# Wide moving operands on four column groups, paired key turns and a new reduction in a decode attention kernel

## The chip, the cores and the metric

The kernel runs on one core of a Trainium2 chip, in one launch. The metric is device time in microseconds; five runs of the kernel before have a median of 196.19 us.

## The reference

One token goes through two branches. Branch A is attention of 32 heads of 128 over the last 4096 positions of a key and a value cache; branch B is a small gated MLP. Both start from the layernorm of x, and every tensor is bf16.

```python
x = A_x                                   # (1, 1, 512)
xn = _layernorm(x)
q = xn @ wq                               # 32 heads x 128
scores = q . k[:, last 4096] * 128**-0.5  # k, v: (32, 32768, 128), the last 4096 rows of each
o = softmax(scores) . v[:, last 4096]
s = o @ wo                                # (4096, 512)
h = gelu(_layernorm(xn) @ w1)
hs = (quarters of h shifted along the sequence, which has length 1, so zeros) @ w2
x1 = xn + hs
h2 = gelu(_layernorm(x1) @ w3) @ w4       # w3 (512, 1376), w4 (1376, 512)
out = x + s * silu(x1 + h2)
```

The keys and values that are needed make 64 MiB of the 78.84 MB that the kernel reads.

## The kernel before

**Groups and rows.** The 32 heads are worked in eight groups g of G = 4 heads. A key or value tile of a group is 128 partitions by CP = 128 rows of 128 values, 4 MB: partition p holds 128 consecutive positions of one of the four heads, and which head it is goes by p modulo 4. A score is thus the product of a row c of partition p with the query of that partition's head.

**Two ways to a score.** VectorE takes the first nd(g) of the 128 rows of a group: it multiplies them with the query, spread over all partitions as q_bc, and sums (k_vector, L329 and L331, in four quarters of nd/4 rows). TensorE takes the rest in batches of up to eight: it transposes each row (k_turn, L345), ScalarE copies the batch out of PSUM (L347), and a matmul of the transposed keys with four queries gives four columns per row (k_scores, L353), of which ScalarE and VectorE pick the one of the partition's own head (sm_own, L362, and sm_max, L367). nd is 64 for groups 0, 1 and 7, 68 for group 3, and 80 for the others.

**Softmax.** The maximum of each partition (L369) is turned into a row (sm_turn, mt_ps, L375), reduced per head (mx, L377), negated into md (L379) and spread back (mb_ps, L384); ScalarE then makes the exponentials pT (L391) and their sums. A matmul with ones adds the sums over partitions (den_ps, L397) and VectorE takes the reciprocal rden (L402).

**Values.** For groups 0 to 6 (MOVED) the values are the moving operand: a matmul takes four rows of pT as 16 stationary columns and four rows of v as 512 moving columns (v_part, L431), at four row offsets of one PSUM tile ov, which a matmul with zeros opens (L427). ScalarE copies ov to SBUF (L435). Of each 16 by 512 block only the parts where the row of pT meets the same row of v count; v_add picks and adds them with eight matmul instructions against the 0/1 matrix fold (L447), and v_out multiplies with rden: on ScalarE (L461) for groups 0 to 4, on VectorE (L457) for the last three. For group 7 v is the stationary operand, one row at a time (L440), in parts as its four loads (cuts 0, 64, 96, 112, 128) arrive.

**Output rows.** The 32 head outputs go through wo in blocks of 16, 8, 4 and 4 heads. ox_spread and ox_pick (L468 to L482) regroup a block so that the rows of wo can lie 4 or more to a partition; y_wide (L495) multiplies the first block in one PSUM row, y_block and y_head (L156) the others into y_ps.

**The front.** The layernorm sums, the MLP (a_ps L236, a_bf, hr_ps L250 and L255) and the queries (qT_ps L271) come first, with the weights as stationary operand for a_ps and qT_ps. w4 is loaded as eight rows to a partition, 32 further rows, and two tiles of 160 rows each (w4_few) on 20 partitions.

**Order.** All loads go down SP's queue in program order: w2, w3, w4, wq, keys 0 to 2, values 0, keys 3, values 1, and so on. Three buffers hold keys (the first 24 rows of wo take one for a time), two hold values, so SP waits for the last reader of a buffer before it issues the next load. Step s of the main loop works the keys of group s, the softmax of group s - 1 and the values of group s - 2 (LAG); v_add of group s - 3 stands in it too. TensorE, VectorE and ScalarE are in a region in which they take their work strictly in the order of the program. In a step, VectorE's order is: quarter 0 of the keys, rden of group s - 2, quarter 1, mx and md of group s - 1, quarters 2 and 3, then the sum and maximum of L367 and L369. All small PSUM tiles of a step (den_ps, mt_ps, mb_ps, oT, ox_ps) share one buffer of ps_misc, so each waits until the one before has been read.

Of the kernel before, what the change touches and what calls it, by code (L numbers as in the profile page):

```python
# [8 lines left out]
P = 128  # L9
BF16 = mybir.dt.bfloat16  # L10
# [11 lines left out]
NE = 5  # L22
# [3 lines left out]
MOVED = (0, 1, 2, 3, 4, 5, 6)  # L26
# [3 lines left out]
def kernel(  # L30
# [28 lines left out]
    assert F == 8 * P + 64 * NE + 32  # L59
# [30 lines left out]
    w4_sb = wts.tile([P, 9, D], BF16, name="w4_sb")  # L90
    load(w4_sb[:, 0:8, :], B_w4[0:8 * P, :].rearrange("(p c) n -> p c n", p=P))
    load(w4_sb[0:32, 8, :], B_w4[F - 32:F, :])
    w4_few = wts.tile([64, 8, D], BF16, name="w4_few")
    nc.gpsimd.memset(w4_few[:], 0.0)
    for c in range(2):
        f0 = 8 * P + 32 * NE * c
        load(w4_few[32 * c:32 * c + 4 * NE],
             B_w4[f0:f0 + 32 * NE, :].rearrange("(b a t) n -> a b (t n)", b=4, a=NE))
# [4 lines left out]
    def load_kv(pool, cache, g, cuts=(0, CP)):  # L103
# [3 lines left out]
        for c0, c1 in zip(cuts, cuts[1:]):  # L107
# [11 lines left out]
    one_f = ones_f[0:1, 0:1]  # L119
    ones_bf = const.tile([P, P], BF16, name="ones_bf")  # L120
    nc.vector.memset(ones_bf[:], 1.0)

    sel = wts.tile([H, H // G, PB, G], BF16, name="sel")
    nc.vector.tensor_copy(out=sel[:], in_=ident_bf[0:H, 0:H].rearrange("k (i a) -> k i a", a=G).unsqueeze(2)
                          .to_broadcast([H, H // G, PB, G]))
# [21 lines left out]


# [33 lines left out]

    few = const.tile([P, 2, 32], BF16, name="few")
    nc.vector.memset(few[:], 0.0)
    for c in range(2):
        nc.vector.tensor_copy(
            out=few[:, c, 0:4 * NE].rearrange("p (a b) -> p a b", b=4),
            in_=ident_bf[:, 4 * NE * c:4 * NE * (c + 1)].rearrange("p (b a) -> p a b", b=4))

# [35 lines left out]
    def w3_cols(c, j):  # L225
        if j < 8:
            return w3_sb[:, c, j:8 * P:8]
        if j == 8:
            return w3_sb[:, c, F - 32:F]
        return w3_sb[:, c, 8 * P + j - 9:8 * P + 64 * NE:8]  # L230

    chunks = [P] * 8 + [32] + [8 * NE] * 8
    a_ps = ps_misc.tile([P, 17], FP32, tag="misc", name="a_ps")
    for j, m in enumerate(chunks):
        for c in range(KC):
            nc.tensor.matmul(a_ps[0:m, j:j + 1], lhsT=w3_cols(c, j), rhs=z3_bf[:, c:c + 1],  # L236
                             start=(c == 0), stop=(c == KC - 1))
    a_bf = small.tile([P, 17], BF16, name="a_bf")
    nc.scalar.activation(out=a_bf[:, 0:8], in_=a_ps[:, 0:8], func=ACT.Gelu_apprx_tanh)  # L239
    nc.scalar.activation(out=a_bf[0:32, 8:9], in_=a_ps[0:32, 8:9], func=ACT.Gelu_apprx_tanh)  # L240
    nc.scalar.activation(out=a_bf[0:8 * NE, 9:17], in_=a_ps[0:8 * NE, 9:17], func=ACT.Gelu_apprx_tanh)
    af_ps = ps_misc.tile([64, 8], FP32, tag="misc", name="af_ps")
    nc.tensor.matmul(af_ps[:], lhsT=few[0:8 * NE].rearrange("p a b -> p (a b)"), rhs=a_bf[0:8 * NE, 9:17],
                     start=True, stop=True)
    af_bf = small.tile([64, 8], BF16, name="af_bf")
    nc.vector.tensor_copy(out=af_bf[:], in_=af_ps[:])

    hr_ps = ps_misc.tile([1, D], FP32, tag="misc", name="hr_ps")
    for c in range(KC):
        nc.tensor.matmul(hr_ps[:], lhsT=shifted_bf[:, c:c + 1], rhs=w2_sb[:, c, :], start=(c == 0),  # L250
                         stop=False)
    for i, m in enumerate(chunks):
        act = a_bf[0:m, i:i + 1] if i < 9 else af_bf[:, i - 9:i - 8]
        w = w4_sb[0:m, i, :] if i < 9 else w4_few[:, i - 9, :]
        nc.tensor.matmul(hr_ps[:], lhsT=act, rhs=w, start=False,  # L255
                         stop=(i == len(chunks) - 1))
    hr = wts.tile([1, D], FP32, name="hr")
    nc.vector.tensor_copy(out=hr[:], in_=hr_ps[:])  # L258
    h2_ps = ps_misc.tile([P, P], FP32, tag="misc", name="h2_ps")
    rows_open(h2_ps)  # L260
    rows_add(h2_ps, one_f, hr, True)
# [6 lines left out]
    qT_ps = ps_misc.tile([P, H], FP32, tag="misc", name="qT_ps")  # L268
    for h in range(H):
        for c in range(KC):  # L270
            nc.tensor.matmul(qT_ps[:, h:h + 1], lhsT=wq_sb[:, c, h * Dh:(h + 1) * Dh],  # L271
                             rhs=xq_bf[:, c:c + 1], start=(c == 0), stop=(c == KC - 1))
    qT_bf = small.tile([P, H], BF16, name="qT_bf")
    nc.vector.tensor_copy(out=qT_bf[:], in_=qT_ps[:])
    qr_ps = ps_misc.tile([H, Dh], BF16, tag="misc", name="qr_ps")
    nc.tensor.transpose(qr_ps[:], qT_bf[:], ident_bf[:])
    q_rows = wts.tile([H, Dh], BF16, name="q_rows")
    nc.vector.tensor_copy(out=q_rows[:], in_=qr_ps[:])
    q_bc = small.tile([P, H // G, Dh], BF16, name="q_bc")
    for i in range(0, H // G, 4):  # L280
        qb_ps = ps_tr.tile([P, 4, Dh], FP32, tag="pt", name="qb_ps")
        for k in range(4):
            nc.tensor.matmul(qb_ps[:, k, :], lhsT=sel[:, i + k, :, :].rearrange("k b a -> k (b a)"),
                             rhs=q_rows[:], start=True, stop=True)
        nc.scalar.copy(out=q_bc[:, i:i + 4, :], in_=qb_ps[:])  # L285
# [29 lines left out]
    def nd(g):  # L315

        return 64 if g < EARLY or g >= LATE else 68 if g == 3 else 80
# [17 lines left out]
    def batches(g):  # L335
        n, m = nd(g), CP - nd(g)
        k = -(-m // 8)
        edges = [n + m * i // k for i in range(k + 1)]
        return list(zip(edges, edges[1:]))

    def k_turn(g, kn, b):
        c0, c1 = batches(g)[b]
        pt = ps_tr.tile([P, 8, P], BF16, tag="pt", name="pt")
        for c in range(c0, c1):
            nc.tensor.transpose(pt[:, c - c0, :], kn[:, c, :], ident_bf[:])  # L345
        kts[b] = kt_pool.tile([P, 8, P], BF16, tag="kt", name="kt")
        nc.scalar.copy(out=kts[b][:, 0:c1 - c0, :], in_=pt[:, 0:c1 - c0, :])  # L347

    def k_scores(g, b):
        kt = kts.pop(b)  # L350
        c0, c1 = batches(g)[b]
        for c in range(c0, c1):
            nc.tensor.matmul(st[g]["sT"][:, c - nd(g), :], lhsT=kt[:, c - c0, :],  # L353
                             rhs=qT_bf[:, G * g:G * g + G], start=True, stop=True)
# [68 lines left out]
    def v_part(g, v, c0=0, c1=CP):  # L423
        s = st[g]
        if g in MOVED:
            s["ov"] = ps_o.tile([P, 4, Dh], FP32, tag="oT", name="ov")
            nc.tensor.matmul(s["ov"][:], lhsT=zero_bf[:], rhs=zero_bf[:].unsqueeze(1).to_broadcast([P, 4, Dh]),  # L427
                             start=True, stop=False, skip_group_check=True)
            for i in range(CP // 4):
# [7 lines left out]
        if c0 == 0:  # L437
            s["oT"] = ps_o.tile([P, G], FP32, tag="oT", name="oT")
# [51 lines left out]
    def y_wide(i, t0, t1):  # L490
        n = blocks[i][1]
        if t0 == 0:
            yr[i] = ps_tr.tile([1, D], FP32, tag="pt", name="yr_ps")
# [146 lines left out]
```

## Time and profile before

| quantity | value |
|---|---|
| median of 5 runs (lowest, highest) | 196.19 us (195.1, 196.34) |
| profiled execution: its own time, its span | 196.3 us, 194.5 us |
| TensorE matmul, weight load, VectorE, ScalarE busy | 136.2, 96.7, 145.4, 90.2 us |
| mean granted clock of TensorE | 0.683 |
| read from memory | 78.84 MB |

Busy time is a sum over the whole span; which engine holds the end is read from the slices (the span in 40 parts of 4.9 us, a digit for the busy tenths), from the chain of work that ended last, and from the timeline of a stretch. In a group's row the columns are the line, engine, operation and tiles, the count, then busy time and mean duration, then idle time ahead of it with what ended it.

### The profile page before, as it was taken

The page shows a single profiled execution, that of the slowest core. Times are in us where ns is not written, and L with a number is a line of the kernel's source. Part 1 is how long each engine was busy: PE and PEld are TensorE (multiplying, and loading weights), DVE is VectorE, ACT ScalarE, POOL GpSimd, SP SyncE. Part 2 cuts the span into 40 slices and gives each one's busy share as a digit, 9 for nine tenths or more (in the row PEclk, how much of TensorE's full clock was granted, in tenths as well). Part 3 has the DMA queues.
Part 4 walks back from the last instruction along what each step waited for, and adds up shares of the span by engine and source line. Part 5 has one row for each costly group of instructions (what it writes and reads, how often), then busy time and mean ns, then how long its engine had stood idle before and what let it go on. Part 6 is the DMA issues. An engine that isn't in the chain of part 4 may idle for free.

```text
span 194.5 us, 3919 instructions
## 1 busy us (share of the span) xinstructions
PE 136.2 (70%) x1696; PEld 96.7 (50%) x1696; DVE 145.4 (75%) x168; ACT 90.2 (46%) x197; POOL 5.9 (3%) x12
## 2 busy tenths in 40 slices
PE   0548978876965169249767891974497989787892
PEld 0447248755855053248437451932493358536281
DVE  0580012999999999998999999999999997942011
ACT  2003002888678265308865850681378157843100
POOL 8210000000000000000000000000000000000000
PEclk9999975695555555855788567578555795855575
DMA  6999999999999999999999999999999999999950
GB/s 205 429 431 425 425 435 435 426 428 425 431 428 433 431 435 431 431 438 431 428 431 431 428 431 408 451 431 431 428 438 433 421 426 391 453 428 406 394 221 0
DMA packets 4722, 79.08 MB, mean 407 GB/s; under 512 B 666, under 2 KB 1210, under 8 KB 1722
## 3 DMA queue, kind: packets, MB, share of 16 engines
q1 hardware_dynamic: 4554, 78.84, 95.3%
q8 instruction: 13, 0.21, 0.4%
q10 hardware_dynamic: 152, 0.00, 0.0%
q14 instruction: 3, 0.02, 0.0%
HBM read 78.84 MB, written 0.00 MB: 405 GB/s over the span
## 4 chain that ended last, share of the span: by engine, by line
DVE 44%; PE 32%; DMA 13%; ACT 5%; issue 4%; POOL 0%; POOLq 0%; ACTq 0%; SPq 0%
DVE S L331 25%; DVE prod L329 14%; DMA kv<-in_A_k_cache_dram 11%; PE ov L431 5%; PE pt L345 4%; PE oT L447 4%; ACT kt L347 3%; PE hr_ps L255 3%; PE a_ps L236 2%; DMA x_bf<-in_A_x_dram 2%; PE yr_ps L495 2%; PE qT_ps L271 2%; PE oT L440 2%; PE sT L353 2%; PE y_ps L156 1%
## 5 line engine op out<-in xcount | busy, mean ns | idle before, releaser
L331 DVE TENSOR_REDUCE S<-prod 128x20 f32<-128x2560 bf16 (+2 forms) x32 | 82.2, 2570 | 1.1
L347 ACT COPY kt<-pt 128x1024 bf16<-128x1024 bf16 (+1 forms) x56 | 54.8, 1008 | 17.4 <-PE pt L345 16.7
L345 PE MATMUL pt<-ident_bf,kv 128*128 128x128 bf16 x444 | 47.7, 279 | 2.9 <-DMA kv<-in_A_k_cache_dram 2.8
L329 DVE TENSOR_TENSOR prod<-kv,q_bc 128x2560 bf16<-128x2560 bf16 (+2 forms) x32 | 43.5, 1360 | 1.8 <-ACT q_bc L285 1.3
L345 PEld LDWEIGHTS <-kv 128*128 128x128 bf16 x444 | 38.7, 128 | 7.5 <-DMA kv<-in_A_k_cache_dram 3.9
L353 PE MATMUL sT<-qT_bf,kt 128*128 128x4 bf16 x444 | 20.8, 169 | 15.0 <-ACT kt L347 14.1
L353 PEld LDWEIGHTS <-kt 128*128 128x128 bf16 x444 | 17.3, 104 | 22.7 <-ACT kt L347 22.4
L431 PE MATMUL ov<-kv,pT 128*16 128x512 bf16 x224 | 24.1, 608 | 0.0
L447 PE MATMUL oT<-fold,ov_sb 128*128 128x4 f32 x56 | 10.7, 315 | 14.5 <-DVE rden L402 13.6
L447 PEld LDWEIGHTS oT<-fold,ov_sb 128*128 128x128 f32 x56 | 10.1, 270 | 15.9 <-DVE rden L402 14.0
L391 ACT ACTIVATE pT<-S,mb 128x128 bf16<-128x128 f32 x32 | 14.0, 579 | 0.3
L431 PEld LDWEIGHTS <-pT 128*16 128x16 bf16 x224 | 6.8, 123 | 14.1 <-issue 13.8
L461 ACT ACTIVATE o<-oT,rden 128x1 bf16<-128x1 f32 x20 | 3.6, 264 | 20.3 <-PE oT L447 20.3
L435 ACT COPY ov_sb<-ov 128x512 f32<-128x512 f32 x7 | 4.1, 585 | 17.0 <-PE ov L431 17.0
L457 DVE TENSOR_TENSOR o<-oT,rden 128x4 bf16<-128x4 f32 x3 | 0.5, 161 | 11.9 <-PE oT L447 9.4
L362 ACT ACTIVATE own<-sT,par 128x48 f32<-128x48 f32 (+2 forms) x32 | 7.6, 360 | 3.6 <-PE sT L353 3.6
L391 ACT ACTIVATION_READ_ACCUMULATOR pT<-S,mb 128x1 f32 x32 | 8.4, 263 | 0.0
L239 ACT ACTIVATE a_bf<-a_ps 128x8 bf16<-128x8 f32 x1 | 0.2, 177 | 14.4 <-PE a_ps L236 14.4
L375 PE MATMUL mt_ps<-ident_f,m 128*1 128x128 f32 x8 | 3.0, 373 | 5.3 <-DVE rden L402 4.4
L258 DVE COPY hr<-hr_ps 1x512 f32<-1x512 f32 x1 | 0.7, 679 | 7.3 <-PE hr_ps L255 7.3
L384 PE MATMUL mb_ps<-md,par_t 5*128 5x4 f32 x16 | 4.1, 325 | 2.7 <-DVE md L379 2.7
L236 PE MATMUL a_ps<-z_bf,w_sb 128*128 128x1 bf16 (+2 forms) x68 | 4.8, 205 | 1.5 <-DVE z_bf L219 1.5
(119 smaller groups left out, 102.8 us busy)
## 6 DMA issues: line engine op xcount, KB each, us to landing
kv<-in_A_k_cache_dram SPq DMA_DIRECT2D x7, 4096.0 KB, 30.9
kv<-in_A_v_cache_dram SPq DMA_DIRECT2D x7, 4096.0 KB, 29.1
wq_sb<-in_A_wq_dram SPq DMA_DIRECT2D x1, 4096.0 KB, 16.3
kv<-in_A_k_cache_dram SPq DMA_DIRECT2D x2, 2048.0 KB, 20.5
wo<-in_A_wo_dram SPq DMA_DIRECT2D x1, 2048.0 KB, 25.8
kv<-in_A_v_cache_dram SPq DMA_DIRECT2D x1, 2048.0 KB, 10.2
w_sb<-in_B_w_dram SPq DMA_DIRECT2D x1, 1376.0 KB
w_sb<-in_B_w_dram SPq DMA_DIRECT2D x1, 1024.0 KB, 9.0
```

Of the source, the lines that this page charges most:

```text
L236: nc.tensor.matmul(a_ps[0:m, j:j + 1], lhsT=w3_cols(c, j), rhs=z3_bf[:, c:c + 1], start=(c == 0), stop=(c == KC - 1))
L255: nc.tensor.matmul(hr_ps[:], lhsT=act, rhs=w, start=False, stop=(i == len(chunks) - 1))
L329: nc.vector.tensor_tensor(out=prod[:, 0:m, :], in0=kn[:, rows, :], in1=q_bc[:, g:g + 1, :].to_broadcast([P, m, Dh]), op=ALU.mult)
L331: nc.vector.tensor_reduce(out=st[g]["S"][:, rows], in_=prod[:, 0:m, :], axis=AX.X, op=ALU.add)
L345: nc.tensor.transpose(pt[:, c - c0, :], kn[:, c, :], ident_bf[:])
L347: nc.scalar.copy(out=kts[b][:, 0:c1 - c0, :], in_=pt[:, 0:c1 - c0, :])
L353: nc.tensor.matmul(st[g]["sT"][:, c - nd(g), :], lhsT=kt[:, c - c0, :], rhs=qT_bf[:, G * g:G * g + G], start=True, stop=True)
L362: nc.scalar.mul(s["own"][:, 0:m, a], s["sT"][:, 0:m, a], par[:, a:a + 1])
L384: nc.tensor.matmul(mb_ps[:], lhsT=par_t[:].rearrange("k b a -> k (b a)"), rhs=md[:], start=True, stop=True)
L391: nc.scalar.activation(out=s["pT"][:, :, a], in_=s["S"][:], func=ACT.Exp, scale=scale, bias=mb[:, a:a + 1], accum_out=s["sum"][:, a:a + 1])
L431: nc.tensor.matmul(s["ov"][r:r + 4 * G], lhsT=s["pT"][:, c:c + 4, :].rearrange("p i a -> p (i a)"), rhs=v[:, c:c + 4, :], start=False, sto ...
L447: nc.tensor.matmul(s["oT"][:], lhsT=s["ov_sb"][:, j, :], rhs=fold[:, G * j:G * j + G], start=(j == 0), stop=(j == 3))
```

## The change

- w4 is loaded as ten rows to a partition and 96 further rows of one; w4_few and its picking matrix go.
- The MLP's products have the activations as the one stationary column and the weights as moving operand of up to 512 columns, at four row offsets (32 apart) of a PSUM tile that a matmul with zeros opens; the gelu is then taken of a row, and the row is turned into columns by three transposes. hr comes in four partial rows, which ind adds.
- Queries likewise: 32 matmuls of 512 columns, copied to q_row; q_bc comes from it by one matmul per four groups. For the keys in pairs, q_row is written twice beside itself, turned as fp32, and stored as q_pair, with zeros in the other key's four columns.
- k_turn reads two neighbouring key rows (2 x 128 bf16) as 128 fp32 values and turns them in one transpose against ident_f. k_scores multiplies the even and the odd halves with q_pair, two matmuls of eight columns for each pair, which add up.
- nd becomes 80 for group 3 and 72 for group 7.
- All groups use the wide form of values. v_add is four fp32 transposes into one ps_misc tile, 124 columns apart, and a reduction on VectorE. Of the last group, the first 64 rows go wide and are folded by v_fold, the rest follow one row at a time.
- Output blocks 0, 1 and 2 go wide at four row offsets; y_four and y_sum hold their partial rows, added through ind at the end.

The diff, cut to its core:

```diff
-    w4_sb = wts.tile([P, 9, D], BF16, name="w4_sb")
-    load(w4_sb[:, 0:8, :], B_w4[0:8 * P, :].rearrange("(p c) n -> p c n", p=P))
-    load(w4_sb[0:32, 8, :], B_w4[F - 32:F, :])
...
-    for c in range(2):
-        f0 = 8 * P + 32 * NE * c
-        load(w4_few[32 * c:32 * c + 4 * NE],
-             B_w4[f0:f0 + 32 * NE, :].rearrange("(b a t) n -> a b (t n)", b=4, a=NE))
+    w4_sb = wts.tile([P, 11, D], BF16, name="w4_sb")
+    load(w4_sb[:, 0:10, :], B_w4[0:10 * P, :].rearrange("(p c) n -> p c n", p=P))
+    load(w4_sb[0:96, 10, :], B_w4[10 * P:F, :])
...
+    def zeros(ps):
+        nc.tensor.matmul(ps, lhsT=zero_bf[:], rhs=zero_bf[:].unsqueeze(1).to_broadcast([P, ps.shape[1], P]),
+                         start=True, stop=False, skip_group_check=True)
...
+    a_ps = ps_misc.tile([P, 3, P], FP32, tag="misc", name="a_ps")
+    zeros(a_ps[:])
     for c in range(KC):
...
+        for j, dst, w in parts:
+            nc.tensor.matmul(dst, lhsT=z3_bf[:, c:c + 1], rhs=w, start=False, stop=(c == KC - 1),
+                             skip_group_check=True)
...
+    for i, (col, w) in enumerate(terms):
+        r = 32 * (i % 4)
+        nc.tensor.matmul(hr_ps[r:r + 1].rearrange("r j n -> r (j n)"), lhsT=col, rhs=w, start=False,
+                         stop=(i >= len(terms) - 4), skip_group_check=True)
...
+    for b in range(2):
+        zeros(qr[b][:])
         for c in range(KC):
...
+            for a in range(G):
+                nc.tensor.matmul(qr[b][32 * a:32 * a + 1], lhsT=xq_bf[:, c:c + 1], rhs=wc[:, 4 * b:4 * b + 4, a, :],
+                                 start=False, stop=(c == KC - 1), skip_group_check=True)
+    nc.scalar.copy(out=q_row[:, 0:4, 0, :], in_=qr[0][:])
+    nc.vector.tensor_copy(out=q_row[:, 4:8, 0, :], in_=qr[1][:])
...
-        return 64 if g < EARLY or g >= LATE else 68 if g == 3 else 80
+        return 64 if g < EARLY else 72 if g >= LATE else 80
...
-        pt = ps_tr.tile([P, 8, P], BF16, tag="pt", name="pt")
-        for c in range(c0, c1):
-            nc.tensor.transpose(pt[:, c - c0, :], kn[:, c, :], ident_bf[:])
-        kts[b] = kt_pool.tile([P, 8, P], BF16, tag="kt", name="kt")
-        nc.scalar.copy(out=kts[b][:, 0:c1 - c0, :], in_=pt[:, 0:c1 - c0, :])
+        n = (c1 - c0) // 2
+        pt = ps_tr.tile([P, 4, P], FP32, tag="pt", name="pt")
+        for i in range(n):
+            c = c0 + 2 * i
+            nc.tensor.transpose(pt[:, i, :], kn[:, c:c + 2, :].rearrange("p c d -> p (c d)").bitcast(FP32),
+                                ident_f[:])
+        kts[b] = kt_pool.tile([P, 4, 2 * P], BF16, tag="kt", name="kt")
+        nc.scalar.copy(out=kts[b][:, 0:n, :], in_=pt[:, 0:n, :].bitcast(BF16))
...
-        for c in range(c0, c1):
-            nc.tensor.matmul(st[g]["sT"][:, c - nd(g), :], lhsT=kt[:, c - c0, :],
-                             rhs=qT_bf[:, G * g:G * g + G], start=True, stop=True)
+        for i in range((c1 - c0) // 2):
+            c = c0 + 2 * i - nd(g)
+            for l in range(2):
+                nc.tensor.matmul(st[g]["sT"][:, c:c + 2, :].rearrange("p c a -> p (c a)"),
+                                 lhsT=kt[:, i, l::2], rhs=q_pair[:, g, l, :], start=(l == 0), stop=(l == 1))
...
+    def v_wide(g, v, c1=CP):
+        s = st[g]
+        for i in range(c1 // 4):
+            c, r = 4 * i, 32 * (i % 4)
+            nc.tensor.matmul(ov[r:r + 4 * G], lhsT=s["pT"][:, c:c + 4, :].rearrange("p i a -> p (i a)"),
+                             rhs=v[:, c:c + 4, :], start=(i < 4), stop=(i >= c1 // 4 - 4),
+                             skip_group_check=True)
+        s["ov_sb"] = sm_pool.tile([P, 4, Dh], FP32, tag="ov_sb", bufs=1, name="ov_sb")
+        nc.scalar.copy(out=s["ov_sb"][:], in_=ov[:])
 
     def v_add(g):
+        s = st[g]
+        ot_ps = ps_misc.tile([P, 4 * P], FP32, tag="misc", name="ot_ps")
+        step = P - 4
+        for j in range(4):
+            nc.tensor.transpose(ot_ps[:, step * j:step * j + P], s["ov_sb"][:, j, :], ident_f[:])
+        s["oT"] = sm_pool.tile([P, G], FP32, tag="oT", name="oT")
+        nc.vector.tensor_reduce(out=s["oT"][:], in_=ot_ps[:].rearrange("p (x m) -> p m x", m=32)[:, 0:G, :],
+                                axis=AX.X, op=ALU.add)
+
+    def v_fold(g):
         s = st[g]
         s["oT"] = ps_misc.tile([P, G], FP32, tag="misc", name="oT")
         for j in range(4):
             nc.tensor.matmul(s["oT"][:], lhsT=s["ov_sb"][:, j, :], rhs=fold[:, G * j:G * j + G],
-                             start=(j == 0), stop=(j == 3))
+                             start=(j == 0), stop=False)
...
+    def y_wide(i, last):
         n = blocks[i][1]
...
+        for t in range(n):
+            r = 32 * (t % 4)
+            nc.tensor.matmul(yr[0][r:r + 1].rearrange("r j n -> r (j n)"), lhsT=ox_blk[i][:, t:t + 1],
+                             rhs=wo_blk[i][:, t, :], start=False, stop=(last and t >= n - 4),
+                             skip_group_check=True)
...
             if s > 1:
                 sm_den(s - 2)
                 sm_rden(s - 2)
-            if h - 1 in MOVED:
+            if h > 0:
                 v_add(h - 1)
                 v_out(h - 1)
-            if s == 7:
-                rows_add(y_ps, one_f, y_row, False)
...
-            y_block(1)
-            v_part(h, v)
+            y_open()
+            y_wide(1, False)
+            v_wide(h, v)
             v_add(h)
             v_out(h)
             ox_spread(2)
         else:
-            v_part(h, v, 0, cuts[1])
+            v_wide(h, v, cuts[1])
             ox_pick(2)
-            y_block(2)
-            for c0, c1 in zip(cuts[1:], cuts[2:]):
+            y_wide(2, True)
+            nc.vector.tensor_tensor(out=y_sum[:], in0=y_four[:], in1=yr[0][:].rearrange("p j n -> p (j n)"),
+                                    op=ALU.add)
+            v_fold(h)
+            v_part(h, v, cuts[1], cuts[2])
+            rows_add(y_ps, ind, y_sum, False)
+            for c0, c1 in zip(cuts[2:], cuts[3:]):
                 v_part(h, v, c0, c1)
             v_out(h)
```

## The prediction, made before the result was known

> **What bounds the kernel now.** I read the slices of the page first, then the chain, then the timeline of VectorE and TensorE from the landing of the seventh key tile on. From the page:
>
> ```profile
> DVE  0580012999999999998999999999999997942011
> DMA  6999999999999999999999999999999999999950
> DVE S L331 25%; DVE prod L329 14%; DMA kv<-in_A_k_cache_dram 11%; PE ov L431 5%; PE pt L345 4%; PE oT L447 4%; ACT kt L347 3%; PE hr_ps L255 3%; PE a_ps L236 2%; DMA x_bf<-in_A_x_dram 2%; PE yr_ps L495 2%; PE qT_ps L271 2%; PE oT L440 2%; PE sT L353 2%; PE y_ps L156 1%
> L345 PE MATMUL pt<-ident_bf,kv 128*128 128x128 bf16 x444 | 47.7, 279 | 2.9 <-DMA kv<-in_A_k_cache_dram 2.8
> L447 PE MATMUL oT<-fold,ov_sb 128*128 128x4 f32 x56 | 10.7, 315 | 14.5 <-DVE rden L402 13.6
> ```
>
> Two things are full at once. The DMA engines are busy from 3 to 187 us, so bytes alone (78.84 MB at about 430 GB/s) hold the end near 188. VectorE is full from 33 to 171. The chain crosses from one to the other at the seventh key tile (group 6), which VectorE reaches just as it lands. The timeline of VectorE from there:
>
> ```profile
> 135.25 1.49 DVE L329 TENSOR_TENSOR prod<-kv,q_bc 128x2560 bf16<-128x2560 bf16 x1 [0.21 <-DMA kv<-in_A_k_cache_dram]
> 139.51 0.17 DVE L402 RECIPROCAL rden<-den_ps 128x4 f32<-128x4 f32 x1
> 139.63 1.49 DVE L329 TENSOR_TENSOR prod<-kv,q_bc 128x2560 bf16<-128x2560 bf16 x1
> 144.23 0.28 DVE L377 TENSOR_REDUCE mx<-mt_ps 1x4 f32<-1x128 f32 x1 [0.26 <-PE mt_ps L375]
> ...
> 158.84 0.18 DVE L402 RECIPROCAL rden<-den_ps 128x4 f32<-128x4 f32 x1 [0.30 <-PE den_ps L397]
> 163.44 0.28 DVE L377 TENSOR_REDUCE mx<-mt_ps 1x4 f32<-1x128 f32 x1 [0.99 <-PE mt_ps L375]
> 171.30 0.28 DVE L369 TENSOR_REDUCE m<-S 128x1 f32<-128x128 f32 x1
> ```
>
> VectorE goes from the reciprocal (L402) straight into its next quarter of keys: nothing stands between them. From group 6's keys to the last row maximum it needs 171.58 - 135.25 = 36.33 us, 1.55 of them idle (0.26 + 0.30 + 0.99). After that the timeline of TensorE shows a tail in which little overlaps:
>
> ```profile
> 139.74 1.87 PE L447 MATMUL oT<-fold,ov_sb 128*128 128x4 f32 x8 [1.94 <-DVE rden L402]
> 173.58 0.37 PE L375 MATMUL mt_ps<-ident_f,m 128*1 128x128 f32 x1 [0.27 <-DVE rden L402]
> 180.39 3.58 PE L431 MATMUL ov<-kv,pT 128*16 128x512 bf16 x32
> 184.66 1.06 PE L447 MATMUL oT<-fold,ov_sb 128*128 128x4 f32 x8 [0.69 <-ACT ov_sb L435]
> 188.37 1.87 PE L440 MATMUL oT<-pT,kv 128*128 128x4 bf16 x64
> ```
>
> **What the Trainium skill says.** *TensorEngine Tiling (Array Packing)*, Key Properties: tiles of the array run in parallel. The trace agrees: the 32 products of L431, each 512 columns wide and 634 ns long when slow, start 0.107 us apart in four row offsets. *DMA: Bandwidth & Descriptors*, "Why a DMA increments its semaphore by 16": a transfer uses the largest number of engines up to 16 that divides its slowest dimension on both sides, the lowest-numbered ones. The two w4_few loads (source dimension 5, 20 partitions) show five semaphore packets each in the DMA records, the other loads 16; after them wq finishes on most engines at 19.3 to 20.0 us and on five at 21.9 to 22.0. *TensorE: Matmul & The Clock Gate*, queue depth: VectorE takes its queue strictly in order; the trace has no VectorE instruction out of program order. The same page, Terms, calls the transpose mode four times faster for fp32. The trace has one fp32 transpose, mt_ps with a single stationary column; the next matmul starts 0.16 us behind it, so at least that form isn't slow.
>
> **The change, part by part.**
>
> *w4 evenly.* The two loads put 2 x 32 KB on five engines; spread out, it is 20 KB on each of 16. Those five lose 44 KB, at 26.9 GB/s (32 KB in 1.22 us) 1.6 us; the others gain 20 KB, 0.75 us. Since the rings never run empty, the skew lives to the end. For group 6's keys the semaphores come at 131.3 to 134.75; the five latest move to about 132 to 133.1, the latest of the others from 133.2 to 133.9. So tiles land some 0.8 us earlier (134.4 for 135.2 as VectorE sees it), and so does the last byte, 188.9 to 188.1.
>
> *Queries and MLP.* MLP products now take 13.1 to 25.9 us (68 of L236 in 4.8, 21 of L250 and L255 in 7.2). On four groups: 20 products of at most 384 columns, about 1.3 us, and 15 of 512, 15 x 0.107 = 1.6, with zeroing 0.4 each and a turn of the row about 1; done by 20. That is hidden by the wq load (about 21 once even). Queries: 32 products x 0.107 = 3.4 slow, half of it at full clock, I take 2.6; two zeroings 0.6, a copy 0.6, a broadcast 0.4, a copy 0.55 (q_bc takes 0.53 now): 26 at the earliest. The first half of group 0's keys lands at 26.9 less 0.8, seen 0.5 later. VectorE's first keys start near 27 instead of 33.45.
>
> *Rows of VectorE.* A quarter of 16 rows takes 3.58 us, 17 rows 3.66, 20 rows 4.3. Group 3 gains 12 rows: step 3 goes from 16.57 us (0.6 idle) to 18.14, as step 4 has it. Group 7 gains 8: 4 x (3.95 - 3.58) = 1.5 us.
>
> *The sum over the parts of a value row, v_add.* Eight L447 matmuls, 1.87 us at slow clock and 1.06 to 1.12 at full, read by ScalarE, become four fp32 transposes of 128 x 128 and a reduction **on VectorE**, placed right behind the reciprocal. The transposes need the one ps_misc buffer, which the denominator holds until that reciprocal has read it. So VectorE stands there with its next quarter of keys queued behind the reduction, waiting for TensorE, in steps 3 to 7. Price: L447's fp32 weight loads stand 0.213 us apart at slow clock. If the 0.16 of a fp32 moving operand hides beside the next load, four cost 3 x 0.213 + 0.37 = 1.0 us; if not, 3 x 0.373 + 0.37 = 1.5; at full clock about 0.65. I take 1.25, between the slow ones. With a reduction of 0.24 (ln_tot 0.16, mx 0.28) and two handovers of 0.06 (rden end to L447) the stop is d = 1.6 us, with bounds 1.0 and 1.85. Four times slower fp32 would make it 2.3 (four operands at 0.43 each); no row excludes that for 128 columns.
>
> *Keys in pairs.* Eight bf16 transposes and eight score matmuls make 1.25 us a batch at slow clock (step 7). Four fp32 ones at 0.213 to 0.373 are 0.85 to 1.5 instead of 0.86, scores and ScalarE's copy (1.0) unchanged. I take nothing for it: in steps 2 to 6 TensorE idles waiting for keys or the reciprocal, and in step 7 it has one batch less. If that cover is gone, 5 batches after the reciprocal cost 3 us.
>
> *VectorE's sum.* Start 27; step 0 to 41.9; step 1 waits for its tile (last semaphore 42.48, less 0.8, seen 0.5 later), 42.2 to 57.3 (15.1); step 2 18.2; steps 3 to 5 18.14 + 18.14 + 18.3 and 3d: 130.1 + 4.8 = 134.9. Group 6 lands at 134.4, so the 6.5 us of earlier start are eaten by longer steps. From there 36.33 + 1.5 - 1.55 (mt_ps is now done before VectorE asks: after the stop it still has a quarter, 4.3 us, TensorE two batches) + 2d = 39.5: the last maximum at 174.4, **2.8 later** than 171.58.
>
> *The tail.* Before, mt_ps came 2.0 behind that maximum, because TensorE was late (its scores, one batch more and the 3.8 of L495, now 2.1). After, it is ready; the reciprocal in VectorE's order follows the maximum, and mt_ps comes 0.3 behind: 174.7, +1.1. From mt_ps to the value products of group 6: v_add 1.87 becomes about 1.4, y_block 0.95 becomes 8 x 0.107, and the zeroing of ov (0.5) goes while that of y_open stands beside the wait for ox: -0.5. Behind those products (3.6 us both times): copy, v_add, 64 value rows as 16 wide products (1.7 slow, 0.9 full, now 1.75), ox, y_wide(2), v_fold (1.06 to 1.87, new), 64 narrow rows (1.8, as now), y_sum (0.6, new, minus y_block(2) 0.6). Added up in order this is 6.2 us at full clock and 7.5 at slow, against 190.24 - 183.98 = 6.26: +0.6.
>
> *SP's queue.* V of group 7 is issued at 172.82, when group 5's value products end, and group 6's V ends on the first engine at 173.92. After, mb of group 6 comes around 168 and V is issued about 172: no gap. A key tile's buffer is freed at about the same time as before.
>
> *Sum:* +1.1 - 0.5 + 0.6 = +1.2 us on a span of 194.5: 195.7. With the 1.8 between span and its own time (196.3), **197.5 us**; that execution stands 0.1 above the median of the five runs. About 0.5% can be told from no change here.
>
> **Rivals.** *Faster:* the stop is cheap (d = 1.0, TensorE at full clock). VectorE then waits for group 6's tile (134.4), ends at 134.4 + 36.28 + 2 x 1.0 = 172.7, mt_ps at 173.0 (-0.6), -0.6 in v_add and y, tail 0: 195.1 us. For it: step 7's L447 ran at 1.12. It decides from d below about 1.2. Against: four of the seven L447 stretches, each behind an idle TensorE, took 1.87. *Four-pass fp32:* d = 2.3, VectorE reaches group 6 at 137.0 and ends at 177.9; 201.8 us. Against it mt_ps. *V's load late:* if pair turning costs 0.3 more a batch, step 7's values end near 174.5 and the rings run dry for about 1.5 us; with the tail that is 199. *No change:* DMA holds both ends; the last byte, 0.8 earlier, is still hidden by the TensorE tail, and gains and stops cancel: 196.4.
>
> **Chances.** Stop as priced: 0.37; V late: 0.08. Four-pass: 0.1. Cheap: 0.3. Cancelling: 0.15. Range 194.3 to 201.5: it leaves out the best of the cheap case and the worst of the four-pass one. Faster 0.3, same 0.15, slower 0.55.
>
> **What would show it.** VectorE's reduction of ot_ps behind L402 with 1.1 to 1.6 us idle before it, five times; first keys at 27; semaphores of each load within 1.5 us; group 6 reached at 134 to 135, last maximum at 174 to 175. Idle below 0.7 us there, or a last maximum before 172.5, would make me wrong.

## The result, and the profile after

The changed kernel takes **197.47 us** (median of 28 runs, 195.95 to 200.84) where the kernel before takes 195.56 (49 runs on the same chips, 194.85 to 197.21). The ratio, which leaves out executions in a slower state that the chip has now and then, is 1.0082, with a 95% interval of 1.0063 to 1.0101: slower by 1.6 us. (The two medians are 1.9 us apart.)

The profiled execution has a span of 196.7 us and 198.54 us as its own time, 1.1 above the median of its kernel. A second profile of the same kernel, called changed_again below, has 194.2 and 195.99, so the two stand on either side of the median. Of the first, VectorE's slices in busy tenths, the lines of its chain, and two rows of its groups:

```profile
DVE  1561169949999999799979997999799979962021
DVE S L326 39%; DVE prod L324 20%; DMA kv<-in_A_k_cache_dram 14%; PE ot_ps L441 4%; PE ov L430 3%; ACT kt L345 3%; DMA x_bf<-in_A_x_dram 2%; PE pt L342 2%; DVE S L367 1%; DVE m L369 1%; PE oT L456 1%; DVE mx L377 1%; PE yr_ps L508 1%; PE sT L353 1%; DVE oT L443 1%
L441 PE MATMUL ot_ps<-ident_f,ov_sb 128*128 128x128 f32 x28 | 7.8, 435 | 27.5 <-DVE rden L402 26.6
L443 DVE TENSOR_REDUCE oT<-ot_ps 128x4 f32<-128x64 f32 x7 | 1.6, 225 | 14.6 <-PE ot_ps L441 14.6
```

VectorE's row was an almost solid run of nines before; now a 7 stands in it about every 20 us, once in each of steps 3 to 7. The chain has moved onto VectorE: the two lines of its keys, 39% of the chain before (25 + 14), are now 59%, and ot_ps, which did not exist, has 4%. The last row names the new stop: the sum of the value rows works 1.6 us in all and waits 14.6 us in all for TensorE's transposes. Five stops of 1.21 us make 6.1 us of this; the rest lies in the tail, where VectorE has nothing else to do. From the landing of the seventh key tile on, the timeline of VectorE (start, duration, line, in brackets the idle time and what ended it):

```profile
135.97 1.48 DVE L324 TENSOR_TENSOR prod<-kv,q_bc 128x2560 bf16<-128x2560 bf16 x1
140.23 0.17 DVE L402 RECIPROCAL rden<-den_ps 128x4 f32<-128x4 f32 x1
141.61 0.22 DVE L443 TENSOR_REDUCE oT<-ot_ps 128x4 f32<-128x64 f32 x1 [1.21 <-PE ot_ps L441]
141.75 1.48 DVE L324 TENSOR_TENSOR prod<-kv,q_bc 128x2560 bf16<-128x2560 bf16 x1
...
174.61 0.29 DVE L369 TENSOR_REDUCE m<-S 128x1 f32<-128x128 f32 x1
```

The first line has no bracket: before, VectorE waited 0.21 us there for the keys and started at 135.25; now they had been there since 134.08, when TensorE began to turn them, and VectorE came 1.9 us later. Between the reciprocal and the next quarter of keys stand 1.52 us, where there were 0.12. The last maximum ends at 174.90, for 171.58 before. In the timeline of TensorE, where the tail follows from it:

```profile
175.04 0.27 PE L375 MATMUL mt_ps<-ident_f,m 128*1 128x128 f32 x1 [2.06 <-DVE rden L402]
...
181.04 3.63 PE L430 MATMUL ov<-kv,pT 128*16 128x512 bf16 x32
...
191.47 0.96 PE L456 MATMUL oT<-pT,kv 128*128 128x4 bf16 x32
```

TensorE, which was late for mt_ps before, now waits 2.06 us for it. The two profiles are 1.5 us apart for mt_ps (173.58 and 175.04) and 2.2 us apart for the end of the last value product (190.24 and 192.43).

### The profile page after: what moved, and what is told of

The parts are those of the page before. It is cut to its first block, busy times and chain, and to the rows that moved or that the text cites. A ratio compares the mean times of both kernels' runs of the same rounds, so it can differ in the third digit from the quotient of the medians.

```text
span 196.7 us, 2914 instructions
## 1 busy us (share of the span) xinstructions
PE 119.1 (61%) x1193; PEld 75.9 (39%) x1193; DVE 150.8 (77%) x174; ACT 90.9 (46%) x200; POOL 2.3 (1%) x11
## 4 chain that ended last, share of the span: by engine, by line
DVE 65%; DMA 16%; PE 13%; ACT 3%; issue 2%; ACTq 0%
DVE S L326 39%; DVE prod L324 20%; DMA kv<-in_A_k_cache_dram 14%; PE ot_ps L441 4%; PE ov L430 3%; ACT kt L345 3%; DMA x_bf<-in_A_x_dram 2%; PE pt L342 2%; DVE S L367 1%; DVE m L369 1%; PE oT L456 1%; DVE mx L377 1%; PE yr_ps L508 1%; PE sT L353 1%; DVE oT L443 1%
## 5 line engine op out<-in xcount | busy, mean ns | idle before, releaser
L326 DVE TENSOR_REDUCE S<-prod 128x20 f32<-128x2560 bf16 (+2 forms) x32 | 84.9, 2653 | 1.1
L345 ACT COPY kt<-pt 128x1024 bf16<-128x1024 bf16 x53 | 51.9, 1012 | 19.8 <-PE pt L342 18.7
L342 PE MATMUL pt<-ident_f,kv 128*128 128x128 f32 x212 | 44.1, 355 | 9.0 <-DMA kv<-in_A_k_cache_dram 8.8
L342 PEld LDWEIGHTS pt<-ident_f,kv 128*128 128x128 f32 x212 | 32.7, 184 | 13.2 <-issue 8.7
L353 PE MATMUL sT<-q_pair,kt 128*128 128x8 bf16 x424 | 19.6, 170 | 16.5 <-ACT kt L345 15.7
L430 PE MATMUL ov<-kv,pT 128*16 128x512 bf16 x240 | 26.3, 615 | 0.0
L441 PE MATMUL ot_ps<-ident_f,ov_sb 128*128 128x128 f32 x28 | 7.8, 435 | 27.5 <-DVE rden L402 26.6
L441 PEld LDWEIGHTS ot_ps<-ident_f,ov_sb 128*128 128x128 f32 x28 | 5.0, 217 | 29.0 <-DVE rden L402 27.0
L443 DVE TENSOR_REDUCE oT<-ot_ps 128x4 f32<-128x64 f32 x7 | 1.6, 225 | 14.6 <-PE ot_ps L441 14.6
L367 DVE TENSOR_REDUCE S<-own 128x48 f32<-128x192 f32 (+2 forms) x8 | 2.9, 364 | 2.8 <-ACT own L362 2.8
L384 PEld LDWEIGHTS mb_ps<-md,par_t 5*128 5x128 f32 x16 | 3.4, 261 | 1.9 <-PE sT L353 0.9
```

The costliest lines, as they stand in the source:

```text
L326: nc.vector.tensor_reduce(out=st[g]["S"][:, rows], in_=prod[:, 0:m, :], axis=AX.X, op=ALU.add)
L342: nc.tensor.transpose(pt[:, i, :], kn[:, c:c + 2, :].rearrange("p c d -> p (c d)").bitcast(FP32), ident_f[:])
L345: nc.scalar.copy(out=kts[b][:, 0:n, :], in_=pt[:, 0:n, :].bitcast(BF16))
L353: nc.tensor.matmul(st[g]["sT"][:, c:c + 2, :].rearrange("p c a -> p (c a)"), lhsT=kt[:, i, l::2], rhs=q_pair[:, g, l, :], start=(l == 0), ...
L367: nc.vector.tensor_reduce(out=s["S"][:, n:CP], in_=s["own"][:, 0:CP - n, :], axis=AX.X, op=ALU.add)
L384: nc.tensor.matmul(mb_ps[:], lhsT=par_t[:].rearrange("k b a -> k (b a)"), rhs=md[:], start=True, stop=True)
```

## The experiments

Ten variants of the two kernels were run, and the change and one variant a second time, each beside runs of the kernel before on the same chip. A plainer way to take the stop out, a second PSUM buffer for all small tiles, could not be measured, in the change or in the kernel before: PSUM has no room for it. The ratios with their 95% intervals:

| kernel | ratio to before | interval |
|---|---|---|
| the change | 1.0082 | 1.0063 to 1.0101 |
| stop_added (before + stop) | 1.0039 | 1.0013 to 1.0065 |
| rows_added (before + rows) | 1.0088 | 1.0053 to 1.0123 |
| before_even (before + loads and MLP) | 1.0079 | 1.0047 to 1.0110 |
| stop_removed | 0.9963 | 0.9939 to 0.9987 |
| rows_back | 0.9960 | 0.9936 to 0.9984 |
| rows_back_stop_removed | 0.9974 | 0.9955 to 0.9993 |
| keys_single | 1.0074 | 1.0047 to 1.0102 |
| tail_narrow, tail_narrow_again | 1.0128, 1.0129 | 1.0090 to 1.0167, 1.0081 to 1.0178 |
| rows_back_skewed | 1.0102 | 1.0071 to 1.0133 |
| stop_removed_rows_first | 0.9995 | 0.9971 to 1.0019 |
| changed_again | 1.0092 | 1.0063 to 1.0122 |

**The stop taken out of the change.** The transposes get one of the three PSUM buffers of turned keys instead of the one that the denominator holds, so they no longer wait for the reciprocal:

```diff
-        ot_ps = ps_misc.tile([P, 4 * P], FP32, tag="misc", name="ot_ps")
+        ot_ps = ps_tr.tile([P, 4 * P], FP32, tag="pt", name="ot_ps")
```

> The changed kernel with the four transposes of a value row written to one of the three PSUM buffers of turned keys, not to the one small buffer, so that they needn't wait for the reciprocal. Theory (VectorE is the bound through the stops): the idle 1.21 us before the reduction falls below 0.2 in steps 3 to 7, VectorE waits for group 6's keys (134.2 instead of 135.97), the last row maximum comes at 170.3 to 170.8 instead of 174.9, and mt_ps at about 172.5: 2 us faster than the changed kernel (ratio to before near 0.998). Rival (the rows alone are too many, or the tail is the loss): less than 0.6 us faster.

Measured: 0.9963, or 0.7 us faster than before and, by the two ratios, 2.3 us (1.2%) faster than the change. VectorE's timeline:

```profile
134.02 1.49 DVE L324 TENSOR_TENSOR prod<-kv,q_bc 128x2560 bf16<-128x2560 bf16 x1 [1.83 <-DMA kv<-in_A_k_cache_dram]
...
138.28 0.17 DVE L402 RECIPROCAL rden<-den_ps 128x4 f32<-128x4 f32 x1
138.37 0.19 DVE L443 TENSOR_REDUCE oT<-ot_ps 128x4 f32<-128x64 f32 x1
...
170.01 0.29 DVE L369 TENSOR_REDUCE m<-S 128x1 f32<-128x128 f32 x1
```

The reduction stands right behind the reciprocal with no bracket, and so in all five steps. VectorE is early again and waits 1.83 us for the seventh key tile, and the last maximum ends 4.6 us earlier than in the change (170.30). The end gains only about half of that, and TensorE's timeline shows why: the tail now runs into the last loads.

```profile
176.41 3.19 PE L430 MATMUL ov<-kv,pT 128*16 128x512 bf16 x32 [0.68 <-DMA kv<-in_A_v_cache_dram]
...
188.68 0.59 PE L155 MATMUL y_ps<-wo_rows,o 128*1 128x128 bf16 x8 [1.28 <-DMA wo_rows<-in_A_wo_dram]
```

**The rows taken out of the change.** The rows of VectorE are those of before, 68 for group 3 and 64 for group 7:

```diff
-        return 64 if g < EARLY else 72 if g >= LATE else 80
+        return 64 if g < EARLY or g >= LATE else 68 if g == 3 else 80
```

> The changed kernel with VectorE's rows as before (68 for group 3, 64 for group 7). Theory: VectorE has 2.6 us less in step 3, of which 1.9 count until it waits for group 6's keys, and 1.6 less in step 7: last maximum near 171.4; TensorE has one batch more, so mt_ps comes near 173.5 instead of 175.0: 1.5 us faster than the changed kernel, level with before. Rival (TensorE is the bound): not faster, or slower by the batch, 1 us.

Measured: 0.9960, as good as without the stop. The stop is still there, at 1.21 us in four steps and 0.75 in one:

```profile
100.42 0.22 DVE L443 TENSOR_REDUCE oT<-ot_ps 128x4 f32<-128x64 f32 x1 [0.75 <-PE ot_ps L441]
...
139.86 0.23 DVE L443 TENSOR_REDUCE oT<-ot_ps 128x4 f32<-128x64 f32 x1 [1.21 <-PE ot_ps L441]
```

TensorE's granted clock was 1.00 around the first of these (99.3 to 100.5 us) and 0.50 around the second, so the stop is longer at the slow clock: with d as the time that the stop adds between the reciprocal and the next quarter of keys, d is 0.94 us in the one and 1.40 in the other.

VectorE reaches group 6 at 134.21 instead of 135.97, and needs 37.35 us from there to the end of the last maximum (171.56) instead of 38.93. The second difference, 1.6 us, is group 7's rows, for which the prediction had 1.5. The first, 1.8, only happens to be near the predicted 1.57 for group 3: step 3 itself is 2.3 us shorter and step 4 has the short stop, but the first keys came late in this execution and step 1 began 0.8 us later. Again the value products at the end wait for their loads:

```profile
186.63 0.59 PE L456 MATMUL oT<-pT,kv 128*128 128x4 bf16 x16 [0.77 <-DMA kv<-in_A_v_cache_dram]
187.77 0.58 PE L456 MATMUL oT<-pT,kv 128*128 128x4 bf16 x16 [0.54 <-DMA kv<-in_A_v_cache_dram]
```

**Both out.** rows_back_stop_removed has both edits.

> VectorE's rows as before and the stop gone as well. Theory: with the rows back the last products already wait for the last value loads (0.77 and 0.54 us), so DMA holds the end and removing the stops adds little: 0 to 0.5 us faster than with the rows back alone. Rival (stops and rows add up): 2 us faster than with the rows back.

Measured: 0.9974, no better than either alone. VectorE, freed of both, waits 3.79 us for the seventh tile, and the value products of group 6 wait 1.83 us for theirs. (The profiled execution stands 1.1 us above the median of its kernel, and its loads are 1.1 us later than those of rows_back from wq on, so the two waits are longer here than in most.)

```profile
135.35 1.49 DVE L324 TENSOR_TENSOR prod<-kv,q_bc 128x2560 bf16<-128x2560 bf16 x1 [3.79 <-DMA kv<-in_A_k_cache_dram]
```

```profile
177.75 3.59 PE L430 MATMUL ov<-kv,pT 128*16 128x512 bf16 x32 [1.83 <-DMA kv<-in_A_v_cache_dram]
```

So the two costs lie on one chain and do not add up. As soon as one is out, the loads hold much of the end, and the other hides behind them.

**The stop put into the kernel before.** v_add alone is exchanged:

```diff
-        s["oT"] = ps_misc.tile([P, G], FP32, tag="misc", name="oT")
+        ot_ps = ps_misc.tile([P, 4 * P], FP32, tag="misc", name="ot_ps")
...
-            nc.tensor.matmul(s["oT"][:], lhsT=s["ov_sb"][:, j, :], rhs=fold[:, G * j:G * j + G],
-                             start=(j == 0), stop=(j == 3))
+            nc.tensor.transpose(ot_ps[:, step * j:step * j + P], s["ov_sb"][:, j, :], ident_f[:])
...
+        nc.vector.tensor_reduce(out=s["oT"][:], in_=ot_ps[:].rearrange("p (x m) -> p m x", m=32)[:, 0:G, :],
+                                axis=AX.X, op=ALU.add)
```

> The kernel before with only the new sum of value rows (four fp32 transposes and a reduction on VectorE behind the reciprocal). Theory: five stops of 1.4 us delay VectorE by 7 us, no earlier start pays for them; some 2 us are hidden by the gap before the last mt_ps and 1 by other waits: 3.5 to 5 us slower than before (ratio 1.018 to 1.026). Rival (TensorE and DMA hold the end): within 0.5 us, or faster by what four transposes save on TensorE.

Measured: 1.0039, only 0.8 us. The expectation counted the stops and left out what they take the place of. VectorE's waits in the kernel before, from its first keys to 176 us (total, times, longest), the largest of them:

```profile
DVE mx L377 <- PE mt_ps L375: 2.6, 5, 1.0
```

and with the stop:

```profile
DVE oT L450 <- PE ot_ps L448: 5.1, 5, 1.2
```

Of the five waits for mt_ps the four inside the steps are gone: while VectorE stands at the stop, TensorE catches up, and mt_ps is done when VectorE asks. Only the last one, 0.47 us long and after the last maximum, is still there. (This profile is of one of the longest of that kernel's runs, so only which waits there are is read from it.) The rest of the gap between 0.8 us and the 3.5 to 5 that were expected is argued, not measured by itself: v_add is shorter in the tail, and the 2.0 us that TensorE was behind the last maximum absorb part of the delay.

**The rows put into the kernel before.** The same line of nd, the other way round.

> The kernel before with only the 20 rows more for VectorE. Theory (VectorE is full from 33 to 171 us): 2.6 us in step 3 and 1.5 in step 7 more, less 0.6 and 1.3 of waits for TensorE and up to 2.0 of the gap before the last mt_ps: VectorE reaches group 6 near 137.2, last maximum at 173.7 to 175, 0.8 to 2 us slower than before. Rival (VectorE has slack): within 0.4 us, or faster by the batch that TensorE saves.

Measured: 1.0088, or 1.7 us, as much as the whole change costs. The last maximum comes 2.3 us later than before and mt_ps 1.4 us later:

```profile
173.64 0.28 DVE L369 TENSOR_REDUCE m<-S 128x1 f32<-128x128 f32 x1
```

```profile
174.97 0.27 PE L375 MATMUL mt_ps<-ident_f,m 128*1 128x128 f32 x1 [0.27 <-DVE rden L402]
```

TensorE is still the later of the two there (mt_ps 1.05 us behind the end of the maximum, where before it was 2.0), which is the difference between 2.3 and 1.4. In that kernel the stop does not exist, so the rows alone suffice to make it slower.

**Keys one at a time.** keys_single is the change with k_turn and k_scores of before (eight bf16 transposes, eight products of four columns).

```diff
-            nc.tensor.transpose(pt[:, i, :], kn[:, c:c + 2, :].rearrange("p c d -> p (c d)").bitcast(FP32),
-                                ident_f[:])
+            nc.tensor.transpose(pt[:, c - c0, :], kn[:, c, :], ident_bf[:])
```

> The changed kernel, but keys turned one row at a time in bf16 as in the kernel before, against queries turned once from q_row. Theory (TensorE waits for keys, the reciprocal or ScalarE's copies in every step, and VectorE holds the end): within 0.4 us of the changed kernel. Rival (pairs lengthen or shorten TensorE's chain to the last softmax): 1 us or more either way.

Measured: 1.0074, against 1.0092 for changed_again on the same chip: no difference. The batches in the timelines of TensorE, eight bf16 rows in keys_single and four pairs in changed_again, at nearly the same place of the last group and both at a granted clock of 0.50:

```profile
167.68 1.01 PE L333 MATMUL pt<-ident_bf,kv 128*128 128x128 bf16 x8
```

```profile
166.70 1.09 PE L342 MATMUL pt<-ident_f,kv 128*128 128x128 f32 x4
```

Half as many instructions take about the same time.

**The loads and the MLP alone.** before_even is the kernel before with the w4 loads and the MLP of the change.

```diff
-    w4_sb = wts.tile([P, 9, D], BF16, name="w4_sb")
+    w4_sb = wts.tile([P, 11, D], BF16, name="w4_sb")
...
+    for i, (col, w) in enumerate(terms):
+        r = 32 * (i % 4)
+        nc.tensor.matmul(hr_ps[r:r + 1].rearrange("r j n -> r (j n)"), lhsT=col, rhs=w, start=False,
```

> The kernel before with only the new w4 loads and the MLP that goes with them. Theory: the five late DMA engines lose 1.6 us, tiles land about 0.8 us earlier, but VectorE reached group 6 only 0.2 us before its keys and TensorE's tail, not DMA, held the end: 0 to 0.5 us faster. Rival (landing times set the end): 0.8 to 1.2 us faster.

Measured: 1.0079, 1.5 us slower instead of a little faster. What was expected up to group 6 is there: VectorE starts its first keys at 27.62 (33.45 before), waits 2.93 us for group 6, and sees it 0.68 us earlier than before, at 134.57:

```profile
134.57 1.49 DVE L316 TENSOR_TENSOR prod<-kv,q_bc 128x2560 bf16<-128x2560 bf16 x1 [2.93 <-DMA kv<-in_A_k_cache_dram]
155.28 1.23 DVE L316 TENSOR_TENSOR prod<-kv,q_bc 128x2048 bf16<-128x2048 bf16 x1 [0.89 <-DMA kv<-in_A_k_cache_dram]
```

Group 7's keys then keep it waiting 0.89, and mt_ps still comes 1.85 us earlier than before (171.73). But the value products of group 6 wait 1.08 us for their tile, the last load ends at 189.50 by the DMA records, 0.6 us later than in before's profile, and the last value product ends at 189.94, only 0.3 earlier. So the earlier maximum gains nothing because the loads hold the end. Why this kernel is even slower is not shown: the profile is of the quickest of its ten runs (195.99), that of before stands 0.7 above its median (196.3), and no line shows the 1.5 us. **That cause stays open.** It matters for the last sentence of the next section.

**A skew that did not come.** rows_back with w4 loaded in two parts, of 96 and of 32 partitions. The second was meant to lie on four DMA engines:

```diff
-    load(w4_sb[:, 0:10, :], B_w4[0:10 * P, :].rearrange("(p c) n -> p c n", p=P))
+    load(w4_sb[0:96, 0:10, :], B_w4[0:960, :].rearrange("(p c) n -> p c n", p=96))
+    load(w4_sb[96:P, 0:10, :].rearrange("p c n -> p (c n)"),
+         B_w4[960:10 * P, :].rearrange("(a b c) n -> a b (c n)", a=4, b=8))
```

> VectorE's rows as before, with 32 of the 128 partitions of w4 loaded over four DMA engines (80 KB each, where an even spread has 20 KB) to bring a skew back. Theory (rings that never empty carry a skew to the end, and here DMA holds the end): the four engines are 60 KB, 2.2 us late; the latest engine is 1 to 1.4 us late anyway, so 1 to 2 us slower than with the rows back. Rival (the skew is absorbed on the way): within 0.4 us.

Measured: 1.0102, where rows_back has 0.9960: the ratios differ by 0.0142, or 2.8 us. The DMA records show that it was no skew. Each of the three loads of w4 has 16 semaphore packets, where the two small loads in the kernel before have five each. Those of wq, the next load, stand at 22.75 to 23.17 us: close together, but about 2.6 us later than in rows_back (20.09 to 20.63). Packets of 10 KB that took 0.39 us there take up to 0.88 us. In the rates of the slices (GB/s, 4.8 us each, rows_back first, then rows_back_skewed) the loss is in the second and third:

```profile
GB/s 196 421 493 435 384 422 437 435 435 432 429 430 432 429 429 435 435 435 432 429 435 435 432 435 405 459 425 435 435 435 434 429 435 367 480 429 405 412 272 4
```

```profile
GB/s 209 344 326 449 376 422 479 424 429 429 419 429 424 433 443 429 429 429 426 429 429 436 426 429 416 449 433 436 436 436 431 426 436 387 478 426 399 413 267 4
```

Why these packets are slow is open. VectorE's first keys follow the delay, in rows_back and in rows_back_skewed:

```profile
27.41 1.23 DVE L324 TENSOR_TENSOR prod<-kv,q_bc 128x2048 bf16<-128x2048 bf16 x1 [3.67 <-DMA kv<-in_A_k_cache_dram]
```

```profile
30.10 1.23 DVE L326 TENSOR_TENSOR prod<-kv,q_bc 128x2048 bf16<-128x2048 bf16 x1 [2.44 <-DMA kv<-in_A_k_cache_dram]
```

They start 2.7 us later; group 6 is then reached 3.2 us later (137.40 for 134.21), and the last maximum ends 3.2 later (174.75 for 171.56). So the run shows that a delay of all loads in the front goes through to the end in full. It says nothing of a skew between engines, and whether the even loads are needed for the gain of rows_back was not tested.

**A narrow tail.** The first 64 value rows of group 7 one at a time, without v_fold:

```diff
-            v_wide(h, v, cuts[1])
+            st[h]["oT"] = ov[:, 0, 0:G]
+            v_part(h, v, 0, cuts[1])
...
-            v_fold(h)
```

> The changed kernel, but the first 64 value rows of the last group go one row at a time as in the kernel before; v_fold and the second copy of ov go. Theory (behind the last row maximum TensorE runs without a gap): v_fold's 0.98 us goes and 64 narrow rows cost the 1.8 us that 16 wide products cost: 1.0 us faster than the changed kernel. Rival (the last value loads hold the end): within 0.3 us.

> The changed kernel with 64 narrow value rows in the last group, beside the changed kernel on the same chip. Theory as before (v_fold's 0.98 us lies on TensorE's gapless tail; the profile had the stretch from the last mt_ps to the last value product 1.3 us shorter): 0.7 to 1.3 us faster than the changed kernel. Rival (the gain doesn't reach the end): within 0.4 us of it.

> The changed kernel itself, on the chip on which the next three run, so that they can be set against it: ratio to before 1.006 to 1.010.

Measured: 1.0128 and 1.0129, against 1.0092 for changed_again beside the second: not faster, and the intervals overlap. In the stretch of 185 to 190 us (busy time and count of TensorE, weight loads, VectorE, ScalarE and GpSimd, then the granted clock, DMA's share, GB/s), first changed_again, then the change's own profile, then tail_narrow_again (the longest of its six runs):

```profile
185.00:190.00 5.00, 4.52 (x103) 3.23 (x101) 1.60 (x6) 0.59 (x1) 0.00 (x0) 1.00 0.52 195
```

```profile
185.00:190.00 5.00, 4.16 (x31) 1.96 (x31) 1.45 (x6) 0.89 (x2) 0.00 (x0) 0.58 0.50 185
```

```profile
185.00:190.00 5.00, 3.83 (x85) 2.77 (x73) 0.91 (x5) 0.59 (x1) 0.00 (x0) 0.50 0.62 225
```

The same kernel had this stretch at a clock of 1.00 in one execution and 0.58 in another; from the end of group 6's value products to that of the last one, the tail is 6.3 us in the first (183.79 to 190.10) and 7.8 in the second (184.67 to 192.43). A difference of 1 us in the tail is smaller than what the clock does to it. Whether narrow products keep the clock low is open.

**One more edit on a version that beats both.** stop_removed with the last rows of wo loaded ahead of the last values, to take away the 1.28 us wait at its end.

```diff
+            load_rows(H - G, G)
...
-            for r, n in ((H - G, 2), (H - 2, 1), (H - 1, 1)):
-                load_rows(r, n)
```

> The changed kernel with the stop removed and the last four rows of wo loaded in one piece ahead of the last values instead of behind them, so that the last output products needn't wait 1.28 us for them. Theory (DMA holds the end, and what stands behind the last byte counts): behind the last values come 16 value rows, the product with the reciprocal and the output products, 1.4 us, instead of half of the output products behind the last of wo, which lands 1.2 us later: within 0.4 us of the kernel with the stop removed, near 0.996 of before. Rival (the wait for wo is a loss in full): 1 us faster than that.

Measured: 0.9995, on another chip than stop_removed's 0.9963. The intervals overlap, and it is not better. The wait for wo is gone, but the first values of group 7 now come later, and their products wait 2.10 us for them (0.31 in stop_removed). stop_removed, rows_back and rows_back_stop_removed stay the versions whose intervals lie below 1, by 0.3 to 0.4%.

## Why the prediction was right

The direction and the mechanism held: stops of VectorE behind the reciprocal and more rows for it eat up the earlier start. That 197.5 meets 197.47 is luck in part. The forecast was 1.2 us on an execution of 196.3; the kernel before has a median of 195.56 over all its runs, and the change costs 1.6 us by the ratio. Some terms were off and others made up for them.

- **The stop.** It is where it was put, in five steps, 1.21 us of idle each. d = 1.52 - 0.12 = 1.40, for 1.6 taken and 1.0 to 1.85 as bounds: the four transposes take 1.12 us at the slow clock, for 1.25. The four-pass rival (d = 2.3) is out. The cheap rival decides from d below about 1.2, and falls with it, but only because TensorE was at the slow clock in all five steps: at the full clock rows_back had d = 0.94 once.
- **The start.** First keys at 26.06 for 27. But step 1 starts at 43.84 for 42.2. The term left out: VectorE waits 2.84 us for ScalarE's own at the end of step 0. TensorE waits 5.95 us for the second half of group 0's keys (32.22), and behind it follow batches at ScalarE's 1.0 us a copy. An early start of VectorE only meets TensorE's share of the keys late.
- **Steps 1 to 5.** 15.08, 18.22, and three times 19.61 us, for 15.1, 18.2, 19.74, 19.74 and 19.9. So group 6 is reached at 135.97 for 134.9: step 0 lost 1.6 us more than predicted, and the shorter stops gave 0.5 back. That is outside the 134 to 135 that the prediction named as its sign. The last maximum ends at 174.90 for 174.4. Against before the ledger up to group 6 is: start -7.4, three stops +4.2, group 3's rows +2.2 (18.2 us for 16.0, both without waits), the wait in step 0 +2.8, waits for mt_ps and keys gone -1.1, which makes the +0.7 that was measured.
- **mt_ps** at 175.04 for 174.7, and from it to the value products 6.0 us, for 6.8 before and 6.3 predicted. The wide tail is 6.3 to 7.8 us by the clock, for 6.2 to 7.5.
- **The loads.** The last byte was predicted at 188.1, after 188.9 before; it is at 188.78 in this profile and 187.89 in changed_again, so the two do not decide it. The loads are even in the front (the semaphores of wq at 20.16 to 20.68, for 19.3 to 22.0 before), but those of group 6's keys are 1.9 us apart again, where the prediction had 1.5 as its sign; why is open. No gap opens for the values of group 7: they are issued at 172.72, and from the first engine's end of group 6's values (174.1) to its next semaphore (179.54) it takes 5.4 us, for 5.8 before. The rival "V's load late" is not seen.
- **Keys in pairs at nothing** was right by keys_single.

Which part made the kernel slower? Undoing the stop or undoing the rows takes 2.3 to 2.4 us off the change, so in this kernel both are needed for its loss; this is shown. Put into the kernel before, they cost 0.8 and 1.7 us, and the even loads with the new MLP 1.5, whose cause is not known. The change's 1.6 us is therefore no sum of single costs, and no run supports a gain from the even loads and the new MLP by themselves.

## What to carry to other kernels

A reduction moved to a full engine that takes its queue in order costs the wait for its producer, here 1.21 us at TensorE's slow clock, much more than its own 0.22 us; look at which buffer the producer needs and who holds it, since another buffer took that wait away without moving an instruction. Two costs on one chain, in front of the same next limit, give the whole gain when either is undone and no more when both are, so price them together and name what holds the end once they are gone. Before an experiment is read as what it was meant to be, look in the records whether it did that: the load meant to be uneven was not. An earlier start of one engine is worth only what the slower partner of the same step lets through.

## What the runs showed of the hardware

- Four fp32 transposes of 128 x 128 take 0.64 to 0.66 us at a granted clock near 1.00 and 1.06 to 1.12 us at 0.50, about the same as eight bf16 ones (0.61 and 1.01). Turning keys in pairs halves the instructions and saves no time of TensorE.
- The granted clock in one and the same stretch of one kernel was 1.00 in one execution and 0.58 in another, and the tails were 6.3 and 7.8 us long. A stop of VectorE behind four such transposes cost 0.94 us at a clock of 1.00 and 1.40 at 0.50.
- The two loads of the kernel before that lie on five engines left these at 21.9 to 22.0 us at the end of wq, when ten others were done by 20.0.
- With w4 loaded in parts of 96 and 32 partitions, the same number of 10 KB packets took up to 0.88 us instead of 0.39, and all 16 engines were about 2.6 us later at the end of wq. The kernel ended 2.8 us later.
